# First head pair of an LSH attention set up in another order and on other engines, and the hash products of q placed right behind the products with v

## The chip, the cores and the metric

The kernel runs on one core of a Trainium2 chip. The metric is the device time of one execution in microseconds (us), lower is better. Three runs of the kernel before gave a median of 518.12 us (517.72 to 518.73).

A core has five engines that run side by side, each through its own list of instructions in order: PE (matrix products into PSUM), DVE (vector work), ACT (activation functions and copies), POOL (vector work that cannot reach PSUM) and SP (which here issues nearly all DMA transfers). They meet only in semaphores: an instruction waits until another engine has done what it needs.

## What is computed

Three layers in a row. The change touches only the first, an attention in which a query sees those keys whose hash falls into the same bucket:

```python
def _attn_ref(q, k, v, proj):              # q, k, v: 2 x 8 x 768 x 64, proj: 64 x 6
    q_bits = (np.einsum('bhsd,dk->bhsk', q, proj) > 0)
    k_bits = (np.einsum('bhsd,dk->bhsk', k, proj) > 0)
    q_bucket = np.sum(q_bits * powers, axis=-1)
    k_bucket = np.sum(k_bits * powers, axis=-1)
    mask = q_bucket[:, :, :, None] == k_bucket[:, :, None, :]
    scores = np.where(mask, scale * np.matmul(q, k.transpose(0, 1, 3, 2)), -1e9)
    attn = np.exp(scores - np.max(scores, axis=-1, keepdims=True))
    attn = attn / (np.sum(attn, axis=-1, keepdims=True) + 1e-09)
    return np.matmul(attn, v)
# then: a mixture of 8 experts, top 1 (1536 tokens, 512 -> 1024 -> 512),
# then: x @ w_in, SoLU, layer norm, @ w_out
```

## The kernel before, in words

**Blocks and units.** The attention takes two heads at a time: 2 batches x 4 head pairs = 8 blocks, n = 0 to 7. A block is 12 units; a unit is 128 queries of one head against all 768 keys, 96 units in all. For unit i the loop emits, in this order: the scores S(i) on PE (`emit_s`: q times k, then the hash rows `cm` times `b`, which push scores of unlike buckets far down; 4 products of 384 columns, with the 6 transposes of the probabilities of unit i-2 woven in, and the two ACT copies that bring those into SBUF), the row maximum on DVE (`emit_max`), the exponential on ACT (`emit_exp`), and at every even unit the products with v of an earlier pair (`emit_pv`, 24 products). The scores have two PSUM buffers, the transposes one buffer each of two kinds.

**Hand-written places.** Everything else is hung on a unit by `at(unit, step, slot=...)`: slot 0 runs after the scores of the unit, slot 1 after its maximum, slot 2 (the default) at its end, behind the products with v if it has any. The emission order is the order on each engine; nothing reorders it. With s0 = 12 (n - 1), the next block n is made ready while block n - 1 runs: `split` cuts q and k into a high and a low half on POOL, `trans` has SP transpose them by DMA, `bits_a` forms the hash products of q or of k on PE (12 products of 384 columns, L542 for q, L544 and L548 for k) in a PSUM tile m, and `bits_b` compares them on DVE (L570) and sends the rows by DMA to `cm` or `b`.

**The tile m** (pool `ps_m`) has one buffer. Before the hash products, `fin_mm` puts the finished output of the last half block into it (L708 to L710, unit s0 + 5), and DVE takes it out in two reads: `fin_l` (L720) in slot 0 of unit s0 + 6 and `fin_x` (L733, result xf) in slot 1 of that unit, behind the maximum. For n = 1 there is no finished output yet. Who next writes m has to wait for the last of these reads.

**The first block** has nothing to hide behind, and `first()` writes its steps out by hand. Of head 0 and head 1 each: q is scaled and rounded to its high half (`q_hi`), the rest is the low half (`q_lo`, or `lo_pool` on POOL for head 1); the same for k (`k_hi`, `k_lo`). PE transposes the halves (`q_t`, `k_t`, `l_t`, all L420), ACT copies q and k out of PSUM, DVE copies the 64 rows of q into `cm` and the low half of k into `b` (L488, L489 for head 0; L513, L514 for head 1). `setup()` turns the 64 x 6 matrix proj (tile pj) into the hash weights pw with 15 short DVE steps (L223 to L239) and 3 POOL copies. Then PE forms hash products and DVE writes the hash rows (`bits_rows`, L554). Four units are reordered so that units 0 and 1 need head 0 alone. Units 0 and 1 carry the rest of head 1 in `later1` and `later2`. The memset that clears unused rows of `cm` (L506) stands on POOL before `setup_late`, a row of small constants, and before the split of block 1. The inputs are loaded by SP in the order q, k of head 0, q of head 1, proj, k of head 1.

Of the kernel before, what the change touches and what calls it, by code (L numbers as in the profile page):

```python
# [21 lines left out]
def kernel(  # L22
# [15 lines left out]
    nc = tc.nc  # L38
# [273 lines left out]
    def attention(es):  # L312
# [28 lines left out]
        def at(i, f, *a, slot=2):  # L341
            bg.setdefault((i, slot), []).append((f, a))
# [66 lines left out]
        def first():  # L409
# [12 lines left out]
            def row(h):  # L422
                return slice(64 * h, 64 * h + 64)
# [7 lines left out]
            def q_hi(h, on_act):  # L431
                if on_act:
                    act.activation(out=tq[:, h, :, h], in_=q_[:, h], func=AF.Copy, scale=QK_S)
                else:
                    dve.tensor_scalar(out=tq[:, h, :, h], in0=q_[:, h], scalar1=QK_S, scalar2=None, op0=ALU.mult)
# [19 lines left out]
            def l_t(h, ps):  # L455
                if h == 0:
                    pe(ps[0:64], lambda s: tl[:, s, 0])
                else:
                    pe(ps, lambda s: tl[:, s].rearrange("p c d -> p (c d)"))
# [13 lines left out]
                nc.tensor.matmul(w[:, 0:128], ident16, ident16, start=True, stop=True)  # L473
            begin(0)
            nc.gpsimd.memset(cm[96:128, :, 0], 0.0)
            q_hi(0, False)
            q_lo(0)
            pq, pk, pl = t16(ps_t, "t0"), t16(ps_t, "t1"), t16(ps_v, "v")
            q_t(0, pq)
            k_hi(0)  # L480
            k_t(0, pk)
            act.copy(out=d["q", 0], in_=pq)
            q_hi(1, True)
            k_lo(0)
            setup()
            l_t(0, pl)
            act.copy(out=d["k", 0], in_=pk)
            dve.tensor_copy(out=d["c", 0][row(0)], in_=d["q", 0][row(0)])  # L488
            dve.tensor_copy(out=d["b", 0][row(0)], in_=pl[row(0)])  # L489
            mq, mk = t32(ps_m, "m"), ps_s.tile([128, 2, 512], F32, tag="s", name="s")[:, 0]  # L490
            bits_mm(0, "q", (0, 1), mq)
            bits_mm(0, "k", (0, 1), mk)
# [10 lines left out]
            k_t(1, pk1)  # L503
            act.copy(out=d["q", 1], in_=pq1)
            act.copy(out=d["k", 1], in_=pk1)
            nc.gpsimd.memset(cm[32:64, :, 1], 0.0)  # L506
            mid = {}

            def later1():
                pl1 = t16(ps_v, "v")  # L510
                l_t(1, pl1)
                bits_rows(0, "q", 1, mq)
                dve.tensor_copy(out=d["c", 1][row(1)], in_=d["q", 1][row(1)])  # L513
                dve.tensor_copy(out=d["b", 1][row(1)], in_=pl1[row(1)])  # L514

            def later2():
                mid["q"], mk1 = t32(ps_m, "m"), t32(ps_v, "v")
# [3 lines left out]
                bits_rows(0, "k", 2, mk1)  # L521
                bits_rows(0, "k", 3, mk1)

            at(0, later1)
            at(1, later2, slot=1)
            at(3, lambda: bits_rows(0, "q", 3, mid["q"]))

# [22 lines left out]
        def bits_rows(n, which, g, m):  # L550
            h, blk = divmod(g, 2)
            x, i, val, cmp = ("c", 0, MASK, ALU.is_ge) if which == "q" else ("b", 1, -MASK, ALU.is_le)
            r = slice(64 - 64 * h, 96 - 64 * h)
            nc.vector.tensor_scalar(out=flat(op[n][x, h])[r, blk * SB:(blk + 1) * SB],  # L554
                                    in0=m[32 * g:32 * g + 32, 0:SB], scalar1=thr[r, i:i + 1],
                                    scalar2=val, op0=cmp, op1=ALU.mult)
# [420 lines left out]
                at(u, fin_mm, j, slot=0)  # L977
        for n in range(1, NP):
            s0 = 12 * (n - 1)
            at(s0 + 7, bits_a, n, "q")  # L980
            at(s0 + 8, bits_b, n, "q", slot=0)
            at(s0 + 8, bits_a, n, "k")
            at(s0 + 9, bits_b, n, "k", slot=0)
        at(90, gather_load)
# [21 lines left out]
        for nm in "qk":  # L1006
            ldt[0, nm] = ld.tile([128, 2, NS, D], F32, tag=nm, name=nm, bufs=1)
        pj = const.tile([64, NBIT], F32, name="pj")
        for h in range(2):
            for nm, src in (("q", q), ("k", k)):  # L1010
                nc.sync.dma_start(out=ldt[0, nm][:, h], in_=src[0, h].rearrange("(p s) d -> p s d", s=NS))
                if h == 1 and nm == "q":
                    nc.sync.dma_start(out=pj, in_=proj)
        warm = sm.tile([128, 1], F32, tag="warm", name="warm", bufs=1)
        nc.vector.memset(warm, 0.0)
        nc.scalar.activation(out=warm, in_=warm, func=AF.Exp)
# [478 lines left out]
```

## Time and profile before

| what | value |
|---|---|
| median of 3 runs | 518.12 us (517.72 to 518.73) |
| the profiled execution | 518.19 us, its span 516.4 us |
| PE busy | 497.0 us, 96% of the span |
| DVE, ACT, POOL busy | 388.7, 319.9, 282.8 us |
| granted TensorE clock | mean 0.997 of full speed |
| maxima L602 | 96, mean 954 ns |
| exponentials L617 | 96, mean 998 ns |

The span is the time from the first to the last instruction of the profiled execution; 1.8 us lie around it. A busy engine is one with an instruction under way, and for PE that is modelled: products are pipelined, so the start times say more than the busy share. The attention runs from 0 to about 240 us, the experts (L1234 and the lines around it) to 383 us, the last layer to the end.

### The profile page before, as it was taken

The numbers are of one execution on the slowest core, as the hardware profiler recorded it, in microseconds if no ns is written. First come the engines' busy times: TensorE is split into PE (matmuls) and PEld (weight loads), VectorE is DVE, ScalarE is ACT, GpSimd is POOL, SyncE is SP. The second block draws the span as 40 slices with busy tenths as digits, with TensorE's granted clock in tenths as the row PEclk, the third lists the DMA queues.
The fourth block names the chain that finished last, engine by engine and source line by source line (L and its number), as shares of the span: only waits on it lengthen the run. The fifth ranks groups of instructions, "written<-read, shape, count | busy, mean of one in ns | idle before, by whom it ended". The sixth has DMA issues, their size and how long they took to land. (4 is left out here: it accounts for less than half of the span.)

```text
span 516.4 us, 12503 instructions
## 1 busy us (share of the span) xinstructions
PE 497.0 (96%) x4716; PEld 384.9 (75%) x4716; DVE 388.7 (75%) x925; ACT 319.9 (62%) x598; POOL 282.8 (55%) x437
## 2 busy tenths in 40 slices
PE   6799999999999999998899999999989999999995
PEld 4578787888888887887899999999974444444443
DVE  7788888888879888777679898879934887755620
ACT  5678787887887788885266576556723455534421
POOL 7999897969879897734266567422012113122131
PEclk9999999999999999999999999999999999999998
DMA  5678969773846675501599999997800245452281
GB/s 183 141 206 188 234 162 230 198 200 80 186 148 103 182 195 132 146 1 43 162 270 279 300 308 258 281 326 278 275 15 0 42 81 79 114 115 62 61 143 41
DMA packets 107182, 83.21 MB, mean 161 GB/s; under 512 B 80624, under 2 KB 89456, under 8 KB 107120
## 3 DMA queue, kind: packets, MB, share of 16 engines
q1 hardware_dynamic: 104816, 76.09, 59.0%
q0 software_dynamic: 2304, 6.31, 3.2%
q8 instruction: 37, 0.61, 0.5%
q14 instruction: 25, 0.20, 0.1%
HBM read 51.43 MB, written 9.97 MB: 119 GB/s over the span
## 5 line engine op out<-in xcount | busy, mean ns | idle before, releaser
L629 PE MATMUL t<-ident,p 128*128 128x128 f32 x576 | 126.0, 275 | 0.5
L617 ACT ACTIVATE p<-s,mx 128x768 f32<-128x768 f32 x96 | 95.8, 998 | 38.8 <-DVE mx L606 24.2
L602 DVE TENSOR_REDUCE mx<-s 128x1 f32<-128x768 f32 x96 | 91.6, 954 | 28.5 <-PE s L592 22.9
L631 ACT COPY pt<-t 128x384 f32<-128x384 f32 x192 | 85.6, 480 | 6.8 <-PE t L629 5.7
L629 PEld LDWEIGHTS t<-ident,p 128*128 128x128 f32 x576 | 77.8, 141 | 15.4 <-ACT pt L631 8.9
L653 PE MATMUL v<-pt,v 128*64 128x128 f32 x1128 | 71.9, 277 | 0.0
L653 PEld LDWEIGHTS v<-pt,v 128*64 128x64 f32 x1128 | 60.6, 137 | 7.7 <-issue 6.8
L131 POOL TENSOR_SCALAR dm<-dm 128x512 f32<-128x512 f32 x16 | 33.5, 2095 | 59.2 <-ACT dm L126 59.1
L1361 PE MATMUL h<-wi,yT 128*128 128x512 f16 x288 | 63.5, 379 | 1.7 <-ACT dm L126 1.7
L1433 PE MATMUL o<-wo,zT 128*128 128x512 f16 (+1 forms) x312 | 63.7, 363 | 0.1
L1234 PE MATMUL a<-hh,wb 128*128 128x224 f16 (+5 forms) x256 | 63.4, 251 | 0.0
L1235 PE MATMUL a<-hh,wb 128*128 128x224 f16 (+5 forms) x256 | 63.4, 251 | 0.0
L1236 PE MATMUL a<-hh,wb 128*128 128x224 f16 (+5 forms) x256 | 63.4, 251 | 0.0
L592 PE MATMUL s<-k,q 128*128 128x384 f16 x192 | 59.0, 329 | 1.0 <-ACT p L617 1.0
L592 PE MATMUL s<-b,cm 128*128 128x384 f16 x192 | 57.2, 326 | 1.4 <-DVE b L554 1.4
L1205 PE MATMUL a<-xw,wa 128*128 128x224 f16 (+5 forms) x224 | 55.2, 249 | 0.3 <-DVE hh L1214 0.3
L1207 PE MATMUL a<-xw,wa 128*128 128x224 f16 (+5 forms) x224 | 55.2, 249 | 0.0
L1206 PE MATMUL a<-xw,wa 128*128 128x224 f16 (+5 forms) x224 | 55.2, 249 | 0.0
L1361 PEld LDWEIGHTS <-yT 128*128 128x128 f16 x288 | 28.1, 98 | 35.6 <-ACT dm L126 1.9
L1433 PEld LDWEIGHTS <-zT 128*128 128x128 f16 x312 | 30.5, 98 | 32.2 <-issue 0.4
L1439 POOL DMA_INDIRECT out_dram<-o,tok x12 | 12.6, 1048 | 53.3 <-issue 42.4
L168 ACT ACTIVATE wb<-raw 128x1024 f16<-128x1024 f32 x24 | 25.3, 1056 | 24.6 <-DMA raw<-in_moe_w_dram 24.6
(273 smaller groups left out, 1015.8 us busy)
## 6 DMA issues: line engine op xcount, KB each, us to landing
raw<-in_moe_w_dram SPq DMA_DIRECT2D x64, 512.0 KB, 6.6
raww<-in_moe_w_in_dram SPq DMA_DIRECT2D x8, 512.0 KB
raww<-in_moe_w_out_dram SPq DMA_DIRECT2D x8, 512.0 KB, 6.4
xs<-raw SPq DMA_DIRECT2D x8, 448.0 KB, 4.1
v<-in_v_dram SPq DMA_DIRECT2D x8, 384.0 KB
q<-in_q_dram SPq DMA_DIRECT2D x6, 384.0 KB
k<-in_k_dram SPq DMA_DIRECT2D x6, 384.0 KB, 5.5
cm<-q SPq DMA_DIRECT2D x14, 96.0 KB, 2.1
```

The source lines that it names most:

```text
L592: nc.tensor.matmul(t[:, c, 0:SB], d[x, h][:, s], flat(d[y, h])[:, c * SB:(c + 1) * SB], start=first, stop=not first)
L602: nc.vector.tensor_reduce(out=mx[:, 0:1], in_=t[:, :, 0:SB], op=ALU.max, axis=AX.XY)
L617: nc.scalar.activation(out=p, in_=s_t.pop(i)[:, :, 0:SB], func=AF.Exp, scale=mx[:, 1:2], bias=mx[:, 2:3], accum_out=sums[j][:, qt, h:h + 1])
L629: nc.tensor.transpose(t[:, g * 128:(g + 1) * 128], p[:, c, g * 128:(g + 1) * 128], ident)
L631: nc.scalar.copy(out=pt[i][:, 3 * c:3 * c + 3], in_=t[:, 0:SB].rearrange("p (g c) -> p g c", g=3))
L653: nc.tensor.matmul(o[64 * h:64 * h + 64], vt[:, h, c], ph[h][:, c], start=(c == 0), stop=(c == NS - 1), tile_position=(0, 64 * h))
L1205: nc.tensor.matmul(ps[:, i, 0:n], w[:, 0, kk, fs], xw[:, 0, kk], start=(kk == 0), stop=False)
L1234: nc.tensor.matmul(ps, w[:, 0, f, ds], hh[:, 0, f], start=(f == 0), stop=False)
L1235: nc.tensor.matmul(ps, w[:, 0, f, ds], hh[:, 1, f], start=False, stop=False)
L1236: nc.tensor.matmul(ps, w[:, 1, f, ds], hh[:, 0, f], start=False, stop=(f == KF - 1))
L1361: nc.tensor.matmul(ps[:, c], yT[:, a, kk, ts], w_i[:, w, kk, c * 512:(c + 1) * 512], start=(kk == 0 and a == 0 and w == 0), stop=(kk == KD ...
L1433: nc.tensor.matmul(ps, zT[:, KF * a + f], w_o[:, w, f, cs], start=(f == 0 and a == 0 and w == 0), stop=(f == KF - 1 and a == 1))
```

## The change

The edits come in two groups. In `first()`: proj is loaded first; `setup()` stands ahead of the halves of q; the high half of head 0's q is made by ACT and that of head 1's q by DVE (the other way round before); the two copies of k's low half into `b` and head 1's copy into `cm` go from DVE to ACT; the memset of `cm` stands in front of `lo_pool` on POOL; head 1's step `later1` moves from slot 2 to slot 0 of unit 0, and in it the first hash rows come behind the copies. In the steady blocks: `bits_a` of q moves from unit s0 + 7 to s0 + 6 and `bits_b` of q from s0 + 8 to s0 + 7; those of k stay.

```diff
--- before.py
+++ after.py
@@ -473,20 +473,21 @@
                 nc.tensor.matmul(w[:, 0:128], ident16, ident16, start=True, stop=True)
             begin(0)
             nc.gpsimd.memset(cm[96:128, :, 0], 0.0)
-            q_hi(0, False)
+            setup()
+            nc.gpsimd.memset(cm[32:64, :, 1], 0.0)
+            q_hi(0, True)
             q_lo(0)
             pq, pk, pl = t16(ps_t, "t0"), t16(ps_t, "t1"), t16(ps_v, "v")
             q_t(0, pq)
             k_hi(0)
             k_t(0, pk)
             act.copy(out=d["q", 0], in_=pq)
-            q_hi(1, True)
             k_lo(0)
-            setup()
+            q_hi(1, False)
             l_t(0, pl)
             act.copy(out=d["k", 0], in_=pk)
             dve.tensor_copy(out=d["c", 0][row(0)], in_=d["q", 0][row(0)])
-            dve.tensor_copy(out=d["b", 0][row(0)], in_=pl[row(0)])
+            act.copy(out=d["b", 0][row(0)], in_=pl[row(0)])
             mq, mk = t32(ps_m, "m"), ps_s.tile([128, 2, 512], F32, tag="s", name="s")[:, 0]
             bits_mm(0, "q", (0, 1), mq)
             bits_mm(0, "k", (0, 1), mk)
@@ -503,15 +504,14 @@
             k_t(1, pk1)
             act.copy(out=d["q", 1], in_=pq1)
             act.copy(out=d["k", 1], in_=pk1)
-            nc.gpsimd.memset(cm[32:64, :, 1], 0.0)
             mid = {}
 
             def later1():
                 pl1 = t16(ps_v, "v")
                 l_t(1, pl1)
+                act.copy(out=d["b", 1][row(1)], in_=pl1[row(1)])
+                act.copy(out=d["c", 1][row(1)], in_=d["q", 1][row(1)])
                 bits_rows(0, "q", 1, mq)
-                dve.tensor_copy(out=d["c", 1][row(1)], in_=d["q", 1][row(1)])
-                dve.tensor_copy(out=d["b", 1][row(1)], in_=pl1[row(1)])
 
             def later2():
                 mid["q"], mk1 = t32(ps_m, "m"), t32(ps_v, "v")
@@ -521,7 +521,7 @@
                 bits_rows(0, "k", 2, mk1)
                 bits_rows(0, "k", 3, mk1)
 
-            at(0, later1)
+            at(0, later1, slot=0)
             at(1, later2, slot=1)
             at(3, lambda: bits_rows(0, "q", 3, mid["q"]))
 
@@ -977,8 +977,8 @@
                 at(u, fin_mm, j, slot=0)
         for n in range(1, NP):
             s0 = 12 * (n - 1)
-            at(s0 + 7, bits_a, n, "q")
-            at(s0 + 8, bits_b, n, "q", slot=0)
+            at(s0 + 6, bits_a, n, "q")
+            at(s0 + 7, bits_b, n, "q", slot=0)
             at(s0 + 8, bits_a, n, "k")
             at(s0 + 9, bits_b, n, "k", slot=0)
         at(90, gather_load)
@@ -1006,11 +1006,10 @@
         for nm in "qk":
             ldt[0, nm] = ld.tile([128, 2, NS, D], F32, tag=nm, name=nm, bufs=1)
         pj = const.tile([64, NBIT], F32, name="pj")
+        nc.sync.dma_start(out=pj, in_=proj)
         for h in range(2):
             for nm, src in (("q", q), ("k", k)):
                 nc.sync.dma_start(out=ldt[0, nm][:, h], in_=src[0, h].rearrange("(p s) d -> p s d", s=NS))
-                if h == 1 and nm == "q":
-                    nc.sync.dma_start(out=pj, in_=proj)
         warm = sm.tile([128, 1], F32, tag="warm", name="warm", bufs=1)
         nc.vector.memset(warm, 0.0)
         nc.scalar.activation(out=warm, in_=warm, func=AF.Exp)
```

ACT at the start of the program (ks: the halves of k, qs: of q, tp: transposes in PSUM, p: probabilities), before:

```order
L442 ACTIVATE ks<-k 128x768
L482 COPY q_197<-tp 128x768
L433 ACTIVATE qs<-q 128x6x64
L487 COPY k_198<-tp 128x768
L442 ACTIVATE ks<-k 128x768
L504 COPY q_273<-tp 128x768
L505 COPY k_274<-tp 128x768
L617 ACTIVATE p,sums<-s,mx 128x768 x2
```

and changed:

```order
L433 ACTIVATE qs<-q 128x6x64
L442 ACTIVATE ks<-k 128x768
L484 COPY q_197<-tp 128x768
L488 COPY k_198<-tp 128x768
L490 COPY b_199<-tp 64x768
L442 ACTIVATE ks<-k 128x768
L505 COPY q_274<-tp 128x768
L506 COPY k_275<-tp 128x768
L512 COPY b_276<-tp 64x768
L513 COPY cm<-q_274 64x768
L617 ACTIVATE p,sums<-s,mx 128x768 x2
```

The high half of q moved to the front, and three copies of 64 rows were added: one ahead of the second ks, two ahead of the first exponential.

DVE from the hash rows of head 0 to the second maximum, before:

```order
L554 TENSOR_SCALAR b_199<-s,thr 32x384 x2
L602 TENSOR_REDUCE mx<-s 128x1
L604 TENSOR_SCALAR mx<-mx 128x1
L606 TENSOR_SCALAR mx<-mx 128x1
L554 TENSOR_SCALAR cm<-tb,thr 32x384
L513 COPY cm<-q_273 64x768
L514 COPY b_275<-tp 64x768
L602 TENSOR_REDUCE mx<-s 128x1
```

and changed:

```order
L554 TENSOR_SCALAR b_199<-s,thr 32x384 x2
L554 TENSOR_SCALAR cm<-tb,thr 32x384
L602 TENSOR_REDUCE mx<-s 128x1
L604 TENSOR_SCALAR mx<-mx 128x1
L606 TENSOR_SCALAR mx<-mx 128x1
L602 TENSOR_REDUCE mx<-s 128x1
```

The hash row moved ahead of the first maximum, and the two copies left DVE.

PE in unit 18 (block n = 2, s0 = 12), from the last product with v, with what each instruction waits for, before:

```order
L653 MATMUL v<-pt_1004,v 64x128
L592 LDWEIGHTS q_419
L592 MATMUL s<-k_469,q_419 128x384 [waits Activation_49]
...
L629 MATMUL t_1095<-ident,p 128x128 x2
L542 LDWEIGHTS pw [waits DMAHW7_49]
L542 MATMUL m<-q_881,pw 32x384 [waits DVE_49]
```

and changed:

```order
L653 MATMUL v<-pt_1004,v 64x128
L542 LDWEIGHTS pw [waits DMAHW7_49,DVE_49]
L542 MATMUL m<-q_881,pw 32x384 [waits PE_49]
...
L542 MATMUL m<-q_883,pw 32x384
L592 LDWEIGHTS q_419
L592 MATMUL s<-k_469,q_419 128x384 [waits Activation_49]
```

The 12 hash products of q, which stood behind the next unit's scores, stand right behind the products with v now, with the wait for DVE's last read of m at their head.

## Rows read from the trace of the kernel before

**Rows 1.** Busy time by stretch: start:end, length, engines' busy us, PEclk, DMA share, GB/s

```profile
10.00:20.00 10.00, 6.34 (x46) 3.62 (x45) 8.79 (x19) 5.57 (x12) 9.27 (x47) 1.00 0.40 89
300.00:320.00 20.00, 20.00 (x222) 20.00 (x220) 17.79 (x23) 13.47 (x19) 14.15 (x12) 1.00 1.01 264
```

**Rows 2.** Timeline of SP: start us, duration us, engine, line, transfer

```profile
0.74 0.41 SPq L1011 DMA_DIRECT2D q<-in_q_dram  x1
2.13 0.58 SPq L1013 DMA_DIRECT2D pj<-in_proj_dram  x1
```

**Rows 3.** Timeline of DVE, first block (in brackets: idle before it, and releaser)

```profile
3.18 0.86 DVE L435 TENSOR_SCALAR qs<-q 128x384 f16<-128x384 f32 x1 [0.72 <-DMA q<-in_q_dram]
4.08 0.56 DVE L438 SCALAR_TENSOR_TENSOR qs<-q,qs 128x384 f16<-128x384 f32 x1
5.13 0.16 DVE L223 COPY db<-pj 64x6 f32<-64x6 f32 x1
6.81 0.17 DVE L239 COPY pw<-db 64x12 f16<-64x12 f16 x1
10.32 0.96 DVE L602 TENSOR_REDUCE mx<-s 128x1 f32<-128x768 f32 x1 [0.68 <-PE s L592]
11.75 0.61 DVE L554 TENSOR_SCALAR cm<-tb,thr 32x384 f16<-32x384 f32 x1
12.67 0.56 DVE L514 COPY b<-tp 64x768 f16<-64x768 f16 x1
13.27 0.96 DVE L602 TENSOR_REDUCE mx<-s 128x1 f32<-128x768 f32 x1
```

**Rows 4.** Timeline of ACT, first block

```profile
5.33 0.80 ACT L482 COPY q<-tp 128x768 f16<-128x768 f16 x1 [0.78 <-PE tp L420]
6.03 0.53 ACT L433 ACTIVATE qs<-q 128x384 f16<-128x384 f32 x1
```

**Rows 5.** Timeline of PE, first block: hash products of head 1, scores of unit 2

```profile
12.41 0.66 PE L542 MATMUL tb<-q,pw 128*32 128x384 f16 x6 [0.88 <-DVE cm L554]
16.54 0.32 PE L592 MATMUL s<-b,cm 128*128 128x384 f16 x1 [0.22 <-DVE b L554]
```

**Rows 6.** Timeline of POOL: the memset that moves

```profile
11.06 1.37 POOL L506 MEMSET cm<- 32x1536 f16 x1
```

**Rows 7.** Timeline of PE: last hash products of k, blocks n = 1 and 2

```profile
32.48 0.54 PE L548 MATMUL m<-b,pw 128*32 128x384 f16 x4
60.56 0.34 PE L548 MATMUL m<-b,pw 128*32 128x384 f16 x4
```

**Rows 8.** Timeline of PE, units 17 to 22 (block n = 2)

```profile
50.67 0.34 PE L592 MATMUL s<-k,q 128*128 128x384 f16 x1
...
51.99 0.23 PE L708 MATMUL m<-rb,xt 128*128 128x160 f16 x1
...
53.88 1.53 PE L653 MATMUL v<-pt,v 128*64 128x128 f32 x24
55.34 0.34 PE L592 MATMUL s<-k,q 128*128 128x384 f16 x1
...
56.75 0.67 PE L542 MATMUL m<-q,pw 128*32 128x384 f16 x12
57.35 0.34 PE L592 MATMUL s<-k,q 128*128 128x384 f16 x1
...
58.76 1.53 PE L653 MATMUL v<-pt,v 128*64 128x128 f32 x24
...
63.68 1.53 PE L653 MATMUL v<-pt,v 128*64 128x128 f32 x24
```

**Rows 9.** Timeline of DVE: last read of m in units 18, 54, 78

```profile
55.03 0.55 DVE L733 TENSOR_TENSOR xf<-m,r 128x384 f32<-128x384 f32 x1
...
139.35 0.55 DVE L733 TENSOR_TENSOR xf<-m,r 128x384 f32<-128x384 f32 x1
...
194.57 0.55 DVE L733 TENSOR_TENSOR xf<-m,r 128x384 f32<-128x384 f32 x1
```

**Rows 10.** Timeline of PE: first product behind those with v, units 54 and 78

```profile
138.98 0.34 PE L592 MATMUL s<-k,q 128*128 128x384 f16 x1
...
194.86 0.34 PE L592 MATMUL s<-k,q 128*128 128x384 f16 x1
```

## The prediction

> **What bounds the kernel now.** I read the busy time by stretch first. In the expert stage PE has no gap (20.00 of 20 us busy at full clock) [rows 1], and the attention's steady part, read from PE's start times, has none either: in block n = 2 one pair of units follows the other at 4.88 us with the hash products of q in it and 4.92 us with those of k (58.76 - 53.88, 63.68 - 58.76) [rows 8]. PE is the bound there; whatever makes it wait is paid in full, and what other engines save is worth nothing. At the start it is the other way: from 10 to 20 us PE is busy for 6.34 us, DVE for 8.79 and POOL for 9.27 [rows 1]. So the two groups of edits have to be priced in two different stages: the first block by the chain DVE - PE - DVE that leads to the first scores, the steady blocks by PE alone. A shift at the end of the first block goes through to the end, since PE is full behind it.
>
> **The first block: what it costs and gives.** *The load.* q of head 0 is used 3.18 - 0.74 = 2.44 us after its issue [rows 2, 3]. If proj takes as long in q's old place, `setup()` can begin at 3.18. Its 15 steps took 6.81 + 0.17 - 5.13 = 1.85 us, so it ends at 5.03, and `q_lo`, which started at 4.08, starts then: 0.95 late. The high half of q on ACT (0.53 us [rows 4]) is done before that, even with q's load some 0.6 later (proj's issue, 0.58 [rows 2]), so the load of q hides behind `setup()`. From the other side proj needed at most 5.13 - 2.13 = 3.0 us, which would make it 1.5 late instead.
>
> Where a page has a price: the Trainium skill, page "DMA: Bandwidth & Descriptors", section "Anatomy of one DMA — SWDGE (gpsimd) path", gives 2.0 us plus bytes at 436 GB/s. For q's 192 KB that makes 2.45 us, an estimate from the page, and the trace's 2.44 agrees although SP issued it; for proj's 1.5 KB it would be 2.0, and the front of the block would come 0.4 us better than I take it.
>
> *Up to the first maximum.* ACT's copy of q moves from 5.33 to 6.28, that of k follows 0.70 behind (6.03 - 5.33 [rows 4]), then the new copy of the low half: 7.68 to 8.48. Its price is that of ACT's copy of the same width, 0.80 [rows 4], against 0.56 on DVE [rows 3]. PE's last hash products of k (0.34 [rows 7]) end near 8.9. DVE then writes three rows of 0.61 (two of k, and the one of q that stood behind the maximum) and starts the first maximum near 10.7 instead of 10.32: 0.4 late.
>
> *Behind it.* Between the first and the second maximum stood a row and two copies, 13.27 - 11.75 = 1.52 us [rows 3]. They are gone from there, so the second maximum starts near 10.7 + 1.4 = 12.1, 1.17 earlier. The rows of head 1, the last scores of unit 2 (16.54 [rows 5]) and all that hangs on them come 1.2 us earlier. Cover: ACT carries three more copies, 2.4 us, before its first exponential, which comes about 1 us late; nobody waits, since unit 2 stands on the second maximum.
>
> Here a rule speaks against the change: the Trainium skill, page "ScalarE: Activation LUTs", section "Rules for kernel authors", wants such plain elementwise work on VectorE, which it calls up to about three times faster. The trace has 0.80 against 0.56, 1.4 times. Were it three times (1.7 us, an estimate from the page), the first copy alone would cost 0.9 more and leave 0.3 of the 1.2.
>
> *What is late next.* Block 1's k. Its last hash products took 0.54 us where those of block 2 took 0.34 [rows 7]: they already waited 0.2 for the transposed low half, which comes from POOL's split through SP. While they wait, its landing sets when PE goes on, so PE is early there by what POOL gains, up to 1.2 + 0.2 = 1.4 where the wait is gone. The memset of 1.37 us [rows 6] moves into an idle stretch of POOL, before `lo_pool`. But `lo_pool` of k needs `k_hi(1)`, which ACT reaches 0.95 + 0.80 - 0.53 = 1.2 later, and part of that POOL had in hand; I take 0.5 of it, between 0 and 1.2. POOL gains 1.37 - 0.5 = 0.87 (0.15 to 1.37), less than 1.4, so it decides: I take **-0.85 us**. Ends: -1.4 (proj in 2 us, POOL's gain in full) and +0.2 (proj in 3 us, POOL's gain eaten).
>
> **The steady blocks.** *Order alone.* A pair in which hash products stand right behind those with v is the k pair, 4.92; the q pair is 4.88. Seven blocks give 7 x 0.04 = +0.28. DVE's comparison of 0.6 us moves with it and is hidden: it falls into the 1.41 us (56.75 - 55.34 [rows 8]) in which PE forms the next scores.
>
> *The new wait.* The products of q write m, and m's last reader is `fin_x` in the same unit, behind that unit's maximum. Before, 1.41 us of scores lay between; now nothing does. That PE really stands there is seen in the first block, where hash products waited 0.88 us for such a read [rows 5], and the handover took 12.41 - 12.36 = 0.05. In unit 18 the products with v are over at 55.34 [rows 8], and `fin_x` ends at 55.03 + 0.55 = 55.58 [rows 9]: 0.24 us. In unit 54 it is 139.90 - 138.98 = 0.92, in unit 78 195.12 - 194.86 = 0.26 [rows 9, 10]. For the six blocks n = 2 to 7 I read 0.24, 0.52, 0.27, 0.92, 0.62, 0.26: 2.83, plus 6 x 0.05 = **3.13 us**. Block 1 has no finished output and does not wait. Behind the waiting products stand the next scores, and behind these DVE and ACT; PE has no slack later to make it good. If DVE were never behind, each wait would still be 0.24 + 0.05, since a maximum and `fin_x` take longer than the products with v: 1.7 us is the lower end, 3.5 the upper (a handover of 0.1 each).
>
> **The sum.** -0.85 + 0.28 + 3.13 = +2.56 on the profiled 518.19, which lies 0.07 above the median: **520.7 us**. By the ends: 518.19 - 1.4 + 0.28 + 1.7 = 518.8, and 518.19 + 0.2 + 0.28 + 3.5 = 522.2.
>
> **The rivals.** *No wait.* DVE, with 1.52 us less to do in the first block and its comparison elsewhere, might run ahead of PE so that m is free in time. Then 518.19 - 0.85 + 0.28 = 517.6: no change. For it: the wait is only a few tenths in four of six blocks. Against it: the maximum begins when the scores end, whatever DVE saved before.
>
> *Faster.* Scores in front of products of full width take 1.32 us (51.99 - 50.67), in front of the narrow hash products 1.41 (56.75 - 55.34) [rows 8]: 0.09 more, perhaps for the change of width. Behind the products with v, which are narrow too, that step would be saved once a block, 7 x 0.09 = 0.63. With no wait and the first block's full 1.4: 518.19 - 1.4 - 0.63 = 516.2. Against it: the k pair already has this order and, at 4.92, is not shorter.
>
> *Slower still: ACT becomes the bound of the first block.* If its three copies push the first exponential past the time at which unit 2 needs the first unit's PSUM buffer, the 1.2 us are lost and turn into some 0.5. It decides from an exponential that starts about 2 us later than now; I count 1. Then 518.19 + 0.5 + 3.41 = 522.1.
>
> **How the numbers follow.** The forecast 0.60, no wait 0.17, faster 0.12, slower still 0.11. The range 517.5 to 522.1 leaves out the faster case and part of the slowest. The forecast's own range is 518.8 to 521.8; a small part of it lies within 0.2% of 518.12 (517.1 to 519.2), about what a measurement of this kernel can tell from no change. So: faster 0.13, same 0.22, slower 0.65.
>
> **What would show it.** Right: in the changed profile the products of q start 0.2 to 0.9 us behind the last product with v, with `fin_x` as releaser, in six blocks and not in the first; q pairs of 5.2 to 5.9 us; the second maximum near 12.1; block 1's k products still waiting. Wrong, if m is free at once (q pairs of 4.92), if the scores of unit 2 end later than 16.5, or if a shift seen at 40 us is gone in the expert stage.

## The result, and the profile of the changed kernel

The changed kernel takes **523.39 us** (median of 6 runs, 522.22 to 524.12), the kernel before, timed beside it, 518.01 (517.72 to 519.00): a ratio of 1.0098, 95% interval 1.0083 to 1.0113, or +5.4 us. The forecast was +2.6 us, 520.7, with a range up to 522.1: the sign is right, the size outside the range. The profiled execution took 522.91 us, its span 521.1. Lines behind the load of proj (1013) stand one lower in the changed kernel, those inside `first()` up to two higher or one lower.

I follow one point through all traces: the start of PE's last full group of 24 products with v, at 237.40 us in the kernel before and 242.75 in the changed one, **+5.35**. So the loss is complete before the experts begin; what follows gives 0.65 of it back (the first product of the last layer is 4.70 later).

*Stretches* of the changed kernel, as in [rows 1] (start:end, length, busy us of PE, PEld, DVE, ACT, POOL, PEclk, DMA share, GB/s):

```profile
10.00:20.00 10.00, 7.52 (x61) 4.61 (x60) 9.14 (x20) 7.91 (x15) 9.10 (x48) 1.00 0.34 69
300.00:320.00 20.00, 20.00 (x219) 20.00 (x217) 19.49 (x25) 12.85 (x18) 13.76 (x13) 1.00 1.02 312
```

PE does more between 10 and 20 us than before (7.52 instead of 6.34), and in the experts it is as full as it was. This is what a first block that runs earlier would look like too, so one has to look at the single steps.

*Steady blocks.* PE in block n = 2, as in [rows 8], and then the products of q of blocks 3 and 5 with the reads of m that release them, as in [rows 9, 10]:

```profile
54.43 1.53 PE L653 MATMUL v<-pt,v 128*64 128x128 f32 x24
56.19 0.67 PE L542 MATMUL m<-q,pw 128*32 128x384 f16 x12 [0.23 <-DVE xf L733]
...
59.64 1.53 PE L653 MATMUL v<-pt,v 128*64 128x128 f32 x24
...
64.65 1.53 PE L653 MATMUL v<-pt,v 128*64 128x128 f32 x24
...
84.68 0.55 DVE L733 TENSOR_TENSOR xf<-m,r 128x384 f32<-128x384 f32 x1
85.28 0.67 PE L542 MATMUL m<-q,pw 128*32 128x384 f16 x12 [1.02 <-DVE xf L733]
...
142.39 0.55 DVE L733 TENSOR_TENSOR xf<-m,r 128x384 f32<-128x384 f32 x1
142.99 0.67 PE L542 MATMUL m<-q,pw 128*32 128x384 f16 x12 [1.42 <-DVE xf L733]
```

The waits of PE and of its weight loads between 20 and 245 us, summed (engine, line, what was waited for: us in total, times, longest):

```profile
PE m L542 <- DVE xf L733: 3.8, 6, 1.4
...
PEld L542 <- DVE xf L733: 5.3, 6, 1.7
```

The wait is there, in six blocks, by `fin_x`, as forecast: the products start 0.05 us behind its end (84.68 + 0.55 = 85.23, 85.28). The q pair of n = 2 takes 5.21 us (59.64 - 54.43) instead of 4.88. Over the blocks 1 to 7 the q pairs are 4.91, 5.21, 6.00, 5.24, 6.41, 5.62 and 5.24 us where they were 4.89, 4.88, 4.89, 4.88, 5.01, 4.89 and 4.88: 4.31 us more.

*First block.* DVE and POOL, as in [rows 3, 6]; ACT, as in [rows 4]; PE, as in [rows 5, 7]:

```profile
2.46 1.37 POOL L475 MEMSET cm<- 32x1536 f16 x1
2.77 1.09 DVE L223 COPY db<-pj 64x6 f32<-64x6 f32 x1 [0.31 <-DMA pj<-in_proj_dram]
5.29 0.17 DVE L239 COPY pw<-db 64x12 f16<-64x12 f16 x1
5.49 0.56 DVE L438 SCALAR_TENSOR_TENSOR qs<-q,qs 128x384 f16<-128x384 f32 x1
5.97 0.55 DVE L446 SCALAR_TENSOR_TENSOR kl<-k,ks 128x384 f16<-128x384 f32 x1
...
11.81 0.96 DVE L602 TENSOR_REDUCE mx<-s 128x1 f32<-128x768 f32 x1
...
13.12 0.95 DVE L602 TENSOR_REDUCE mx<-s 128x1 f32<-128x768 f32 x1
```

```profile
6.97 0.80 ACT L484 COPY q<-tp 128x768 f16<-128x768 f16 x1 [1.52 <-PE tp L420]
...
8.38 0.80 ACT L490 COPY b<-tp 64x768 f16<-64x768 f16 x1
...
13.79 0.99 ACT L617 ACTIVATE p<-s,mx 128x768 f32<-128x768 f32 x1
```

```profile
6.11 0.82 PE L420 MATMUL tp<-ident,qs 128*128 128x128 f16 x6 [1.51 <-DVE qs L438]
...
8.27 1.09 PE L542 MATMUL tb<-q,pw 128*32 128x384 f16 x6
...
14.92 0.32 PE L592 MATMUL s<-k,q 128*128 128x384 f16 x1 [1.01 <-ACT p L617]
...
16.38 0.32 PE L592 MATMUL s<-b,cm 128*128 128x384 f16 x1 [0.20 <-DVE b L554]
...
33.22 0.34 PE L548 MATMUL m<-b,pw 128*32 128x384 f16 x2 [0.55 <-DMA b<-kl]
```

Two things were not forecast. DVE's first step of `setup()`, 0.16 us in [rows 3], takes 1.09, and the second 1.02: both end when POOL's memset, which runs beside them, is over (2.46 + 1.37 = 3.83; they end at 3.86 and 3.87). And PE's transposes and hash products take up to 0.85 and 1.09 us where they took 0.50 to 0.66. The last scores of unit 2 come only 0.16 earlier (16.38 against 16.54), and block 1's k products wait longer than before for the low half: 0.55 us of idle stand in front of the last two of the four in [rows 7], which begin at 33.22, in the kernel before at 32.7.

### The profile page after: what moved, and what is told of

Its sections match the earlier page's. It is cut to its first block, busy times and chain, and to the rows that moved or that the text cites. A ratio compares the mean times of both kernels' runs of the same rounds, so it can differ in the third digit from the quotient of the medians.

```text
span 521.1 us, 12508 instructions
## 1 busy us (share of the span) xinstructions
PE 498.7 (96%) x4716; PEld 385.3 (74%) x4716; DVE 389.5 (75%) x922; ACT 322.6 (62%) x601; POOL 284.2 (55%) x437
```

## The experiments

The kernel before was timed beside each kernel. "Last v" is the point named above, against 237.40 us.

| run | us | before | ratio (95%) | last v, shift |
|---|---|---|---|---|
| changed kernel | 523.39 | 518.01 | 1.0098 (1.0083 to 1.0113) | +5.35 |
| e1 front only | 518.43 | 517.97 | 1.0005 (0.9992 to 1.0019) | +0.96 |
| e2 steady only | 522.56 | 517.97 | 1.0086 (1.0070 to 1.0102) | +4.85 |
| e3 last read of m first | 519.40 | 517.97 | 1.0025 (1.0015 to 1.0035) | +1.86 |
| e4 front, 54 warm-ups | 518.10 | 517.97 | 0.9997 (0.9984 to 1.0010) | +0.32 |
| e5 front, memset late | 517.55 | 518.21 | 0.9993 (0.9980 to 1.0006) | -0.61 |
| e6 the same, 32 warm-ups | 516.87 | 518.21 | 0.9982 (0.9971 to 0.9994) | -0.81 |
| e7 front, copies on DVE | 518.94 | 518.21 | 1.0013 (1.0004 to 1.0022) | +0.26 |
| e8 steady, DVE work moved | 527.92 | 518.21 | 1.0180 (1.0157 to 1.0203) | +8.69 |
| e9 steady, POOL work moved | 522.63 | 520.68 | 1.0063 (1.0036 to 1.0090) | +2.98 |
| e10 as e1, one profile | 524.31 | 520.68 | | +1.00 |
| e11 best first block | 519.43 | 520.68 | 0.9978 (0.9952 to 1.0004) | -1.63 |
| e12 the same again | 516.35 | 518.22 | 0.9962 (0.9943 to 0.9982) | -1.40 |

Beside e9 to e11 the kernel before took 520.68 us instead of some 518; of these three the traces up to 245 us say more than the times. The single execution of e10 stood 3.1 us in one wait in the experts (for hh, DVE) that e1's does not have.

### Which group costs

e1 takes the steady blocks of the kernel before, e2 the first block of the kernel before:

```diff
# e1, against the changed kernel
-            at(s0 + 6, bits_a, n, "q")
-            at(s0 + 7, bits_b, n, "q", slot=0)
+            at(s0 + 7, bits_a, n, "q")
+            at(s0 + 8, bits_b, n, "q", slot=0)
# e2, against the kernel before
-            at(s0 + 7, bits_a, n, "q")
-            at(s0 + 8, bits_b, n, "q", slot=0)
+            at(s0 + 6, bits_a, n, "q")
+            at(s0 + 7, bits_b, n, "q", slot=0)
```

> The changed kernel with the hash products of q back in their old places (units s0 + 7 and s0 + 8): the edits of the first block alone. Theory (the wait for m in the steady blocks costs 4.3 to 4.8 us, the first block some +0.5 by block 1's first product with v at 36.35 against 35.80 us): 518.0 + 0.5 = 518.5 us, between 518.2 and 519.0, and q pairs of 4.89 us again. Rival (the first block is what costs, by more than its own times show): 520 us or more. My sum before the result (-0.85): 517.2 us.

> The kernel before with the hash products of q in their new places alone (units s0 + 6 and s0 + 7), the first block untouched. Theory (products of q wait for the last read of m in six blocks, 4.3 us, and 0.2 to 0.5 more around them): 522.3 to 522.8 us, q pairs of blocks 2 to 7 between 5.2 and 6.4 us. My term before the result (0.28 + 3.13): 521.4 us. Rival (most of the loss comes out of the first block and only shows up later): 519 us or less.

Measured: +0.46 and +4.59 us, 5.05 together, where the whole change costs 5.38. In e2 the q pairs are 4.92, 5.22, 6.00, 5.23, 6.40, 5.62 and 5.24, to 0.01 those of the changed kernel; in e1 they are 4.88 or 4.89 again, but for 5.03 in block 5 (5.01 in the kernel before). So the steady blocks hold nearly the whole loss, and the first block, which I had at -0.85, gives nothing: by its interval e1 is between -0.4 and +1.0 us.

### Is it the wait, or the order?

e3 is e2 with the last read of m ahead of the maximum in the units that matter:

```diff
-                at(u + 1, fin_x, j, slot=1)
+                at(u + 1, fin_x, j, slot=0 if j % 2 else 1)
```

> The kernel before with the hash products of q in their new places, and the last read of m put ahead of the maximum of unit s0 + 6 instead of behind it (slot 0), so that m is free by the time the products with v are over. Theory (the wait for m is the whole loss of the steady blocks): q pairs of 4.92 us, 518.0 + 7 x 0.04 = 518.3 us, up to 518.8 if the maximum, 0.55 us later in these units, delays the next pair. Rival 1 (it is the order, narrow products behind narrow ones and then wide scores, that costs): 521 us or more, as without this edit. Rival 2 (the scores behind the products with v are now cheaper, or DVE gains slack): 517.4 us or less.

Measured: 519.40, and in the waits of its trace `fin_x` no longer stands before the products of q. Of 4.59 us 3.16 are gone: the wait is the cause, and rival 1 falls. But the time is 0.6 above what I expected at most. The q pairs are 4.92, 4.91, 5.35, 4.91, 5.74, 4.99 and 4.91: blocks 3 and 5 still lose, now further on. PE's next scores wait there for an exponential (PE's scores in block 5; 0.39 of the 0.83 us that this pair is longer than the free ones):

```profile
142.11 0.32 PE L592 MATMUL s<-k,q 128*128 128x384 f16 x1 [0.39 <-ACT p L617]
```

These are the blocks in which the wait for m was longest too (1.09 and 1.49 us; 0.30 to 0.71 in the others), so something makes DVE late there.

### Why blocks 3 and 5 are worse

DVE has additional work shortly ahead of m's read in these blocks: a bit mask of weights (`wide_a`, L136, and `wide_c`, L142) at unit 28, routing (`route_a`, L762) at unit 52. e8 is e2 with this work moved behind the read; e9 is e2 with DVE's work in place and POOL's splitting of a weight piece (`w_split`), which runs beside it, moved:

```diff
# e8, against e2
-        for x, f, g in ((4, route_a, 0), (9, route_mm, 0), (10, route_b, 0), (10, route_s, 0),
+        for x, f, g in ((7, route_a, 0), (9, route_mm, 0), (10, route_b, 0), (10, route_s, 0),
-(12, 19, 20, 28, 28, 34, 35, 40)
+(12, 19, 20, 31, 31, 34, 35, 40)
# e9, against e2
-            at(s0, w_split, *pc)
+            at(s0 + 3 if x in (4, 8) else s0, w_split, *pc)
```

> The kernel before with the hash products of q in their new places, and two pieces of DVE work that stand up to two units ahead of m's last read put behind it: wide_a and wide_c from unit 28 to 31, route_a of part 0 from unit 52 to 55. In blocks 3 and 5 PE waited 1.09 and 1.49 us for m, in the other four 0.30 to 0.71. Theory (there DVE is late by this work, and by 0.5 us each since an operation of it is held up by POOL's beside it): q pairs of blocks 3 and 5 at 5.2 to 5.4 instead of 6.00 and 6.40 us, the others as they were, and 522.56 - 0.7 - 1.1 = 520.8 us. Rival (the work is only moved, and PE loses the same in the next pairs): 522.3 us or more, the loss in the pairs behind.

> The kernel before with the hash products of q in their new places, and POOL's splitting of two weight pieces moved three units back (from units 28 and 52 to 31 and 55), DVE's work left where it is. Theory (POOL's operations of 1.05 us run beside DVE's bit mask L136 and its three short steps L762 and hold them until they end, which is the 0.5 us by which PE waits longer in blocks 3 and 5 than I forecast): L136 at 0.42 to 0.5 us instead of 0.98, L762 at 1.3 or less instead of 1.83, q pairs of blocks 3 and 5 at 5.5 and 5.9 instead of 6.00 and 6.40, 522.56 - 1.0 = 521.6 us. Rival (they are longer for another reason, or DVE waits elsewhere): pairs of 6.0 and 6.4, 522.3 us or more.

In e8 my theory missed by far: 527.92 us. The q pairs of blocks 3 and 5 do fall, to 5.24 and 5.60, but the k pair of block 3 rises to 5.85 (4.91 in e2) and that of block 5 to 8.06 (4.96): the rival's "only moved", and worse; block 6's q pair grows too, to 6.19 (5.62). In block 5 the routing now comes so late that PE stands 2.74 us for m in front of the routing's own products, behind a hash comparison (L570) that DVE reaches late, and when PE goes on, its 24 products with v take 2.83 us instead of 1.53. Products of PE, and the stretch in which they lie:

```profile
151.40 0.17 PE L781 MATMUL m<-oh_all,upper 128*128 128x24 f16 x1 [2.74 <-DVE raw L570]
...
153.18 2.83 PE L653 MATMUL v<-pt,v 128*64 128x128 f32 x24
```

```profile
153.20:154.00 0.80, 0.80 (x9) 0.80 (x10) 0.73 (x3) 0.80 (x3) 0.00 (x0) 0.50 0.22 54
154.00:155.00 1.00, 1.00 (x14) 1.00 (x12) 0.64 (x9) 1.00 (x3) 0.39 (x2) 0.50 0.11 25
```

The granted clock (the third number from the end) fell to 0.50, 1.2 GHz, after that standstill; the 1.3 us are what the lower clock cost on these 24 products.

e9 hits the cause. DVE's steps in e2, with POOL's operations beside the mask and beside `route_a`, and then the steps in e9:

```profile
79.02 0.98 DVE L136 TENSOR_SCALAR db<-dm 128x512 int32<-128x512 int32 x1
80.03 1.40 DVE L142 SCALAR_TENSOR_TENSOR db<-raww,db 128x512 int32<-128x512 int32 x1
...
136.53 1.83 DVE L762 SCALAR_TENSOR_TENSOR rne<-lt,rmx,iota_s 128x8 f32<-128x8 f32 x3
...
165.97 1.37 DVE L762 SCALAR_TENSOR_TENSOR rne<-lt,rmx,iota_s 128x8 f32<-128x8 f32 x3
...
78.67 1.05 POOL L208 TENSOR_SCALAR raw<-raw 128x1024 f32<-128x1024 f32 x1
...
137.30 1.05 POOL L209 TENSOR_SCALAR wa<-raw 128x1024 f16<-128x1024 f32 x1
```

```profile
78.59 0.42 DVE L136 TENSOR_SCALAR db<-dm 128x512 int32<-128x512 int32 x1
79.04 0.69 DVE L142 SCALAR_TENSOR_TENSOR db<-raww,db 128x512 int32<-128x512 int32 x1
135.33 0.50 DVE L762 SCALAR_TENSOR_TENSOR rne<-lt,rmx,iota_s 128x8 f32<-128x8 f32 x3
...
163.33 1.62 POOL L378 TENSOR_SCALAR ks<-k 128x768 f16<-128x768 f32 x2
163.60 1.89 DVE L762 SCALAR_TENSOR_TENSOR rne<-lt,rmx,iota_s 128x8 f32<-128x8 f32 x3
```

The mask takes 0.42 instead of 0.98 us, `wide_c` 0.69 instead of 1.40, the three steps of `route_a` 0.50 instead of 1.83, and the q pairs are 4.92, 5.22, 5.24, 5.24, 5.25, 6.14 and 5.25. Blocks 3 and 5 have become like the others. In block 6 POOL now runs beside the routing's second part (L762 1.89 instead of 1.37), and its pair is longer by the same 0.52 (6.14 against 5.62). The attention ends 1.87 us earlier than in e2. The time does not show it: in e9's trace PE stands idle for 1.07 us between 340 and 380 us, in e2's it does not, and the rest is not explained. So each block pays some 0.32 us for the wait itself, 1.9 in six blocks. Of the other 2.35 of the 4.25 us, e9 takes away 1.91 (0.76 in block 3, 1.15 in block 5) by taking POOL from beside DVE; that block 6's 0.39 is DVE standing behind POOL too is argued from the lengths of L762 there.

The mechanism is in the rows: in e2 the mask starts at 79.02 while POOL's L208 runs (78.67 to 79.72) and ends at 80.00, 0.28 behind it. The Trainium skill, page "SBUF — State Buffer", section "SBUF: two separate sides", says that DVE and GpSimd share one pair of ports, which the instruction that starts first holds to its end, and names two cases: a DVE operation in a 2-port mode, or one with two SBUF inputs, the latter only against a GpSimd operation that reads SBUF. The traces agree: `wide_c` and L762, with two inputs, are held beside POOL's reading operations, while `k_lo` of the changed kernel (L446, two inputs, from 5.97) took its 0.55 us beside POOL's second memset, which ran from 5.63 to 7.00. The mask has one SBUF input, so by that section it would have to run in a 2-port mode, which no trace shows.

### The first block

Four kernels change e1, the first block alone: e4 has 54 instead of 24 warm-up products (products ahead of the transposes whose results nobody uses), e5 the memset of `cm` behind `setup()`, e6 that and 32 warm-up products, e7 the copies of 64 rows on DVE and head 1's step in its old place and order.

```diff
# e4, against e1
-            for _ in range(24):
+            for _ in range(54):
# e5, against e1; e6 has range(32) as well
-            nc.gpsimd.memset(cm[96:128, :, 0], 0.0)
             setup()
+            nc.gpsimd.memset(cm[96:128, :, 0], 0.0)
# e7, against e1
-            act.copy(out=d["b", 0][row(0)], in_=pl[row(0)])
+            dve.tensor_copy(out=d["b", 0][row(0)], in_=pl[row(0)])
...
-                act.copy(out=d["b", 1][row(1)], in_=pl1[row(1)])
-                act.copy(out=d["c", 1][row(1)], in_=d["q", 1][row(1)])
                 bits_rows(0, "q", 1, mq)
+                dve.tensor_copy(out=d["c", 1][row(1)], in_=d["q", 1][row(1)])
+                dve.tensor_copy(out=d["b", 1][row(1)], in_=pl1[row(1)])
-            at(0, later1, slot=0)
+            at(0, later1)
```

> The first block's edits alone, with 54 instead of 24 warm-up products ahead, so that PE stays busy until the first transposes. In the changed kernel PE is idle for 1.51 us ahead of them, and three groups of transposes took 0.82 to 0.85 us instead of 0.50 to 0.60, the first hash products 1.09 instead of 0.66. Theory (PE is slower because it was idle): transposes of 0.5 to 0.6 us again, the first maximum some 0.3 to 0.6 us earlier than without, and up to 0.5 us off the time: 518.0 to 518.4 us where the edits alone give 518.5. Rival (they are slow for what they wait for, one group behind the other): the same 0.8 us and the same time.

> The first block's edits alone, with POOL's memset of 32 rows of cm put behind setup() instead of ahead of it. Theory (DVE's first two steps of setup() take 1.0 to 1.2 us instead of 0.16 because POOL's memset of 1.37 us runs beside them and holds what both use): the two steps take 0.16 us again, setup() ends near 4.55 instead of 5.46, the first transposes start near 5.2 instead of 6.11, and the block comes up to 0.9 us earlier: 517.6 to 518.4 us where the edits alone gave 518.43. Rival (the steps wait for proj's data, or it is a start-up cost of DVE): the two steps stay at 1.0 us or more, and 518.4 us stays.

> As e5_memset_late, and with 32 instead of 24 warm-up products, so that PE stays busy up to the transposes, but not past them as with 54 (which delayed them to 7.17 us). Theory (two separate losses, the held DVE steps and the slow PE behind its idle time): transposes at 5.2 to 5.3 us that take 0.5 us, the first maximum near 10.2 to 10.9, the second near 11.5 to 12.2 us (13.27 in the kernel before), 516.9 to 517.9 us. Rival (block 1 waits for POOL's split and SP's transfers anyway): the maxima come early, block 1's k products wait longer, and the time is that of e4_front_warm, 518.1 us.

> The first block's edits alone, with one part undone: the three copies of 64 rows are DVE's again, and head 1's step stands in its old place with the old order in it; proj first, setup() first and POOL's memset stay as changed. Theory (the copies are worth what I took, 1.4 us less between the first and the second maximum and 0.85 us more ahead of the first): the first maximum near 11.5 instead of 12.35, the second near 14.4 instead of 13.66, and 0.2 to 0.8 us more than the edits alone: 518.6 to 519.2 us. Rival (ACT's load behind the copies eats it: the first exponential came 1.97 us later than before): the same time as the edits alone, 518.4, or less.

> The same program as e1_front_only, profiled once more. In the profiles so far the first transposes took 0.82 to 0.85 us with 1.51 us of idle PE ahead (changed kernel, edits alone), 0.51 with the same idle time (e7), and 0.84 with none (e6). Theory (whether PE runs at full or half speed there differs from one execution to the next, not by kernel): the six transposes and the first hash products differ from those of e1 (0.82, 0.85, 0.85, 1.14, 0.85 us) in at least one group by 0.3 us or more. Rival (the program decides it): within 0.05 us of e1 in every group.

*The held steps.* In e5 the first step of `setup()` takes 0.16 us and the last starts at 4.45 instead of 5.29; the transposes follow at 5.26 instead of 6.11. e5 is 517.55 us, 0.9 below e1, and its attention ends 1.57 earlier (0.61 ahead of the kernel before). For the held steps the theory holds. Of the 1.57 us it explains the 0.84 by which `setup()` ends earlier; e5's transposes were also shorter, for the reason below. The times alone, with intervals that overlap, would not settle it.

*The slow transposes.* My theory was idle time. The first three groups of six transposes (L420) took in us, and the trace's first record of the clock, always at full speed, begins at:

| run | idle ahead | q | k | low half | first clock record |
|---|---|---|---|---|---|
| before | none shown | 0.60 | 0.50 | 0.52 | 4.92 |
| e3, first block as before | none shown | 0.82 | 0.62 | 0.52 | 5.55 |
| e2 and e9, first block as before | none shown | 0.82 | 0.85 | 0.85 | 7.74 |
| changed | 1.51 | 0.82 | 0.85 | 0.85 | 9.17 |
| e1 | 1.51 | 0.82 | 0.85 | 0.85 | 11.18 |
| e10 | 1.51 | 0.82 | 0.85 | 0.84 | 10.54 |
| e7 | 1.51 | 0.51 | 0.50 | 0.52 | 4.54 |
| e5 | 0.66 | 0.51 | 0.51 | 0.52 | 4.99 |
| e4 | none shown | 0.50 | 0.50 | 0.52 | 6.69 |
| e6 | none shown | 0.84 | 0.85 | 0.71 | 7.09 |

PE in e7, fast behind the idle time, and in e6, slow without any:

```profile
6.10 0.51 PE L420 MATMUL tp<-ident,qs 128*128 128x128 f16 x6 [1.51 <-DVE qs L438]
```

```profile
5.25 0.84 PE L420 MATMUL tp<-ident,qs 128*128 128x128 f16 x6
```

The views print a clock of 1.00 also for the time ahead of the first record, which no record covers; there it says nothing. In every trace the slow products end where that record begins. In the changed kernel the hash products of q, from 8.27, take 1.09 us and those of k, from 9.20, take 0.49, with the record from 9.17; in e1 those of k still take 0.85, and head 1's transposes from 10.42 still 0.82, with the record from 11.18. So PE was at the lower of its two clocks, 1.2 GHz, until the clock rose; for the time ahead of the record this is read from the durations, which are a factor of 1.7 apart.

What decides the moment stays open. It is not the program alone: e1 and e10 are one program, and e7 is the same up to the transposes, yet the clock rose at 11.18, 10.54 and 4.54. (PE had then been at work from 1.86 on in e7, with the warm-up products, and in e1 and e10 once more from 6.11 on.) So it is not idle time alone either. But all three rises later than 7.74 us come behind the 1.51 us of idle time, while e7's clock had risen before it, so idle time may delay a rise that has not come yet; four executions do not show it. The rise costs something only where PE stands in the chain: e2, with the first block of the kernel before, had the slow transposes as well, and its first maximum starts at 10.32 like that of [rows 3]; in the changed first block it starts at 11.81, and in e1, with the later rise, at 12.35.

e10 did not differ from e1 by the 0.3 us that I had asked for in the five groups named (0.82, 0.85, 0.84, then 1.14 and 0.85 us for the hash products of q and k). Behind them it did: its clock fell again to 0.50 from 17.37 to 20.78 us, and the pair with block 1's q products starts at 26.76 instead of 26.18. e4 has 0.5 us again, but its 54 products hold PE until 7.17 and so delay the transposes themselves.

*The copies.* e7 shows their worth. Its first maximum starts at 10.78 and its second at 13.71, 2.93 apart; in the changed kernel it is 1.31 (13.12 - 11.81). The second comes in e1 at 13.66. So the copies' 1.5 us between the maxima are gained. The first maximum comes 1.57 later in e1 (12.35), but how much of that the copies cost is not shown, since e7's clock rose 6.6 us earlier. In time e7 is 518.94 against 518.43, with intervals that overlap.

### A first block that is faster

e11 is e6 with POOL's second memset back in its old place, the first copy back on DVE and ACT's `k_hi(1)` ahead of it; e12 is the same program again.

```diff
# e11, against e6
-            nc.gpsimd.memset(cm[32:64, :, 1], 0.0)
...
             act.copy(out=d["k", 0], in_=pk)
+            k_hi(1)
...
-            act.copy(out=d["b", 0][row(0)], in_=pl[row(0)])
+            dve.tensor_copy(out=d["b", 0][row(0)], in_=pl[row(0)])
...
-            k_hi(1)
...
+            nc.gpsimd.memset(cm[32:64, :, 1], 0.0)
```

> A try at a faster first block: e6_memset_warm, with POOL's second memset of cm back behind lo_pool, so that DVE's high half of q (1.38 us beside that memset) takes 0.64 to 0.86 us again, the first of the three copies back on DVE, and ACT's high half of k ahead of it. Theory (the edits of the first block are worth something once DVE and POOL do not stand in each other's way): hash products of head 1 and both maxima some 0.4 to 0.9 us earlier than in e6 (10.96 and 12.27 us), 516.0 to 516.7 us where e6 gave 516.87. Rival (POOL's chain to block 1, 0.3 us later here, then decides): block 1's k pair above 4.92 by what the front gained, 516.9 us or more.

> The program of e11_front_best timed again beside the kernel before: there both kernels ran some 2.5 us above their other times (the kernel before 520.68), and the comparison stayed open, while the profile had the attention end 1.63 us earlier than in the kernel before (242.55 against 244.18 us) and 0.83 earlier than e6 (243.38). Theory (the first block's gain reaches the end, since PE is full behind it): 518.1 - 1.6 - 0.4 = 516.1 us, between 515.7 and 516.8. Rival (the gain is given back before the end): 517.5 us or more.

DVE's high half of q in e6, and in e12 the same and the two maxima:

```profile
6.32 1.38 DVE L435 TENSOR_SCALAR qs<-q 128x384 f16<-128x384 f32 x1 [0.32 <-DMA q<-in_q_dram]
```

```profile
6.73 0.36 DVE L435 TENSOR_SCALAR qs<-q 128x384 f16<-128x384 f32 x1 [0.73 <-DMA q<-in_q_dram]
...
10.34 0.96 DVE L602 TENSOR_REDUCE mx<-s 128x1 f32<-128x768 f32 x1 [0.19 <-PE s L592]
...
11.65 0.95 DVE L602 TENSOR_REDUCE mx<-s 128x1 f32<-128x768 f32 x1
```

The high half takes 0.36 us instead of 1.38 in e6 beside the memset, the second maximum starts 1.62 us earlier than before (13.27 [rows 3]), the attention ends 1.40 earlier, and the time is **516.35 us**, ratio 0.9962 (0.9943 to 0.9982): with the steady blocks left as they were, it beats both kernels. Part of the traces' difference between e6 and e12 is the clock, which rose at 7.09 and at 5.42; the times are medians of 12 executions each.

## Why the prediction was right in sign and wrong in size

**What held.** PE is the bound of the steady part, and a wait there is paid to the end: e2 alone reproduces 4.59 of 5.38 us. The wait's place, its releaser, its absence in block 1 and the handover of 0.05 us are as written. "No wait" and "faster" fell.

**The order alone, +0.28.** Block 1, which doesn't wait, has a q pair of 4.91 instead of 4.89, and with the wait removed e3's free blocks have 4.91 to 4.99: 7 x 0.03 = 0.2. Right.

**The wait, 3.13 us: the term that was too small.** It measures 4.25 (0.30, 1.09, 0.33, 1.49, 0.71, 0.33 for blocks 2 to 7). Four of the six values are within 0.1 of mine; blocks 3 and 5 are 0.5 longer each (0.57 and 0.97 with the handover). The failed step is that I read `fin_x`'s end from the trace of before and let DVE's steps ahead of it keep their length. POOL's operation now starts half a microsecond later against DVE's: 0.35 us ahead of the mask instead of 0.85. The mask grew from 0.48 to 0.98 us, the routing steps from 1.32 to 1.82; before, then changed:

```profile
77.40 1.05 POOL L208 TENSOR_SCALAR raw<-raw 128x1024 f32<-128x1024 f32 x1
...
78.25 0.48 DVE L136 TENSOR_SCALAR db<-dm 128x512 int32<-128x512 int32 x1
...
134.21 1.32 DVE L762 SCALAR_TENSOR_TENSOR rne<-lt,rmx,iota_s 128x8 f32<-128x8 f32 x3
```

```profile
78.87 1.05 POOL L208 TENSOR_SCALAR raw<-raw 128x1024 f32<-128x1024 f32 x1
...
79.22 0.98 DVE L136 TENSOR_SCALAR db<-dm 128x512 int32<-128x512 int32 x1
...
136.74 1.82 DVE L762 SCALAR_TENSOR_TENSOR rne<-lt,rmx,iota_s 128x8 f32<-128x8 f32 x3
```

I also took the 0.92 in unit 54 as it stood, when most of it was already POOL's hold (1.32 us for steps that take 0.50 alone in e9: 0.82). My upper end, 3.5, allowed for a slower handover only, not for DVE's steps becoming longer.

**The first block, -0.85 us: wrong.** It measures +0.46 by e1 (-0.4 to +1.0). The changed kernel's own trace shows where: the pair with block 1's q products starts 0.15 us early (25.64 against 25.79), and behind block 1's k pair (5.80 against 5.12) PE is 0.55 late. So the step that failed is that PE would be early there by what POOL gains.
- *`setup()` behind the load of proj.* It could begin at 2.77, better than my 3.18; but it ended at 5.46 instead of 5.03, because the two first steps were held by the memset of `cm` that I had read only for what it does on POOL. This was the cost of 0.9 us that the sum lacked, and e5 takes it away.
- *First maximum near 10.7.* It came at 11.81: 0.4 from the later `setup()`, the rest from PE's slow transposes and hash products, which I had at their old durations; the clock rose at 9.17 instead of 4.92, and in this order of steps PE stands in the chain. (The 0.70 that I took from 6.03 - 5.33 in [rows 4] is the step from the copy of q to the half of q behind it, not to the copy of k; it came out at 0.69, 7.66 - 6.97.)
- *From the first to the second maximum, 1.4.* 1.31 against 2.95: right in mechanism and size. With the first so late, the second came at 13.12 instead of 12.1.
- *POOL's gain, 0.87.* The split of block 1 starts 0.22 earlier (15.96 against 16.18): `k_hi(1)` came 1.95 later (9.08 against 7.13), where I took 1.2. And what POOL gained did not pass SP: its copies of the transposed q to `cm` (L400) waited longer for q's transposes to land (issued at 23.34 instead of 22.63), and the transposes of k's low half stand behind them. These are issued 0.62 late (L406 below), and block 1's k products waited longer than before. Why q's transposes landed later, though issued 0.22 earlier (18.92), stays open. In e4, e6 and e7 the k products wait no longer than the other blocks' (pairs of 4.91 to 4.93), and e2 has a pair of 5.45 where e3 and e9, with the same first block, have 4.98 and 4.99: this row varies by itself, so part of the 0.68 may be chance.
- *Rival, ACT as the bound.* Its condition was nearly met: the first exponential is 1.97 us later (13.79 against 11.82), and PE stood 1.01 us for it at 14.92. But DVE's rows end last behind it (16.38), so it was not what decided.

SP's queue, the transposes of the low half of block 1's k, before and then changed:

```profile
26.67 2.65 SPq L406 DMA_TRANSPOSE b<-kl  x2
```

```profile
27.29 2.57 SPq L406 DMA_TRANSPOSE b<-kl  x2
```

Together: 4.6 us in the steady blocks where I had 3.4, and about +0.5 in the first where I had -0.85. The range's upper end, 522.1, was near the sum with both at their worst (522.2) and missed by 1.3 us.

## What to carry to other kernels

A wait added to the engine that is the bound costs what the releasing engine's chain takes in the new timing, not in the old one: list what each short operation ahead of the release runs beside on other engines, and price it at its held length as well as its free one. Before work is moved to the front of an engine, look at what its neighbour does at that moment; a memset that nobody waits for can still hold the first steps of a chain. And split a change of two groups at once: here one group cost 0.9%, and the other, rearranged, gained 0.4%.

## What the runs showed of the hardware that I had not expected

- A DVE step of 0.16 to 0.42 us that starts while POOL works on SBUF may end only when POOL's operation is over, 0.03 to 0.28 us behind it: 0.16 became 1.09 beside a memset, 0.36 became 1.38 beside another, 0.42 became 0.98 beside an operation of 1.05 us. Three routing steps of 0.50 together became 1.83.
- PE at half a granted clock after a standstill of 2.74 us (0.50 in the stretches from 153.2 to 155), while the waits of up to 1.49 us in the changed kernel left it at 1.00. A long standstill is not needed: e10's clock fell at 17.37, where the longest wait of PE shown in the 6 us before is 1.01 us.
- PE begins the program at the slow level, and the moment at which it becomes fast differs between executions of one program (11.18 and 10.54 us in e1 and e10): the same six transposes take 0.50 or 0.85 us. The first clock record, not the 1.00 that the views print ahead of it, tells which.
